# An agent-attention and maxout kernel: a rebuilt head, paired key-value additions, five relu slots, halved tiles and a newly searched instruction order

## The chip, the cores and the metric

The kernel runs on one core of a Trainium2 chip. Its time is device microseconds (us) of one execution. Before the change three runs gave a median of 438.29 us (437.61 to 439.87).

The core has five engines, each with its own in-order instruction queue: PE (matrix multiply; its weight loads are listed as PEld), ACT (activations), DVE (element-wise work), POOL (here: casts and additions in SBUF) and SP, which here only issues transfers (DMAs). PE writes into PSUM, which has 8 banks of 128 partitions x 512 fp32; ACT and DVE read from there.

## The reference, cut to what matters

```python
# q, k, v: (4, 12544, 128) fp32;  agents: (4, 49, 128);  w1, w2, w3: (128, 768);  w_out: (768, 128)
def _attn_ref(q, k, v, agents):
    scale = 1.0 / np.sqrt(q.shape[-1])
    def sm(a, b):                       # softmax over the last axis
        ...
    a2k = sm(agents, k)                 # 49 agents attend to 12544 keys
    agent_v = a2k @ v                   # (4, 49, 128)
    q2a = sm(q, agents)                 # each query attends to 49 agents
    return q2a @ agent_v
def _moe_ref(x, w1, w2, w3, w_out):
    h = np.maximum(np.maximum(x @ w1, x @ w2), x @ w3)
    return h @ w_out                    # x is the attention output, 50176 rows
```

## The kernel before, in words

**The algebra.** Each output row is a softmax mixture of 49 agent values, so the kernel multiplies agent values and weights once per batch: G = agent_v @ [w3-w1, w2-w1, w1 @ w_out], and then works from the 49 exponentials of a query instead of its 128 channels. With u = x(w3-w1) and v = x(w2-w1), max(xw1, xw2, xw3) = xw1 + max(relu(u), v). The part xw1 goes straight to the output through w1 @ w_out (the *linear* part).

**The head.** G of batch 0 must exist before any query can pass. The 98 key tiles and 98 value tiles (each 128 rows x 128) of batch 0 come in 12 chunks: ten of 9 tiles, two of 4 (`FIRST`). For chunk g the steps are `kl0.g` and `vl0.g` (loads, issued by SP), `kc0.g` (cast of the keys, POOL), `kt0.g` (transposes on PE into a PSUM pair, as 9 x 128 bf16 columns exceed one bank), `ke0.g` (out of PSUM, DVE), `ks0.g` (scores, PE), `kx0.g` (exp, ACT), `to0.g` (totals, PE), `vc0.g` (cast of the values, ACT), `kv0.g` (exponentials times values, PE, accumulated in one bank). Then `rs0`, `rc0`, `nr0` normalise the agent values into `avT` (DVE), the weights' differences `d31a` and so on are formed (DVE), `gpa` to `gpd` multiply (PE) and `gva` to `gvd` bring the pieces of G out of PSUM (two on ACT, two on DVE). `wm` and `wn` are matmuls of the identity with itself that compute nothing and keep PE busy.

**The stages.** 49 stages s of 8 query tiles (1024 queries) follow: `ql` (load), `qc` (cast, POOL), the transpose (either `qd`, a transposing DMA on SP, for the stages in `TURNED`, or `qt` on PE and `qe` on DVE), `sc` (scores), `ex` (exp on ACT into a tile EQ), `su` and `re` (sums and reciprocals). For each of the six 128-wide slices f of the hidden layer, `u.s.f` (PE) fills a pair of banks, `a.s.f` is its relu (ACT, into an SBUF slot of class AS, of which there are 3), `v.s.f` (PE) fills a second pair and `x.s.f` takes the maximum with AS into a tile of class R (DVE). For f = 4 (`FI`) both steps are on ACT and v is accumulated onto u's own pair. `p.s.o.f` multiplies R with w_out into two output banks, `li.s` adds the linear part, `ov.s.o` scales it into OS (DVE), `st.s` stores it. Where `SPLIT` has a `u`, u's tile is made in two single banks and its relu is two half instructions.

**Batches 1 to 3.** Their keys and values are handled in chunks of 9 tiles while the stages of the batch before run; there POOL casts both, SP turns the keys by DMA (`kt`), and `kv` adds its product into the same bank that holds the chunk's scores; `va` (DVE) adds this into an SBUF sum, once for each of 11 chunks.

**What sets the order.** `graph` lists all steps with their dependencies. The string `ORDER` lists them again in the order in which each engine's queue gets them, with the slot numbers (PSUM bank, SBUF buffer) after a slash. `Plan.waits` derives the semaphore waits from it. An engine that waits holds all that stands behind it in its queue. Every instruction is recorded in one helper, so every row of the profile has the line L388; rows are told apart by their tiles.

## Time and profile before

| | |
|---|---|
| time, median of 3 runs | 438.29 us (437.61 to 439.87) |
| profiled execution, first to last instruction | 436.6 us |
| that span below the median time | 1.7 us |
| PE, DVE, ACT, POOL busy | 94%, 89%, 90%, 39% |
| mean granted TensorE clock | 0.996 |
| DMA moved | 122.37 MB, mean 280 GB/s |

The page gives no device time for the profiled execution itself; its span lies 1.0 us below the fastest run. Names in a row read output<-input (`R<-ps,AS`: tile R is written from PSUM and AS), then the shape, the count, busy time and the mean of one. In a timeline row the numbers are the start and the duration in us, and a bracket tells how long the engine was idle before and what ended this. Under the heading of waits, a row tells who waited, for whose work, the total in us, how many times, and the longest.

### The profile page before, as it was taken

How to read it: one execution, taken by the hardware profiler on the slowest of the kernel's cores; microseconds unless marked ns; L12 is line 12 of the kernel's file. 1: busy time of each engine (PE TensorE's matmuls, PEld its weight loads, DVE VectorE, ACT ScalarE, POOL GpSimd, SP SyncE). 2: the span in 40 equal slices, each digit the busy share in tenths (PEclk: the TensorE clock that was granted, in tenths of full speed). 3: DMA queues.
4: the chain of work that ended last, by engine and by line, in shares of the span. 5: the costliest groups of instructions: out<-in, count | busy, mean ns of one | idle time of the engine just before them, and what ended most of it. 6: DMA issues, size and time to landing. Idle time of an engine off the chain costs nothing.

```text
span 436.6 us, 14853 instructions
## 1 busy us (share of the span) xinstructions
PE 411.9 (94%) x6488; PEld 256.9 (59%) x6488; DVE 386.6 (89%) x470; ACT 393.9 (90%) x486; POOL 170.0 (39%) x177
## 2 busy tenths in 40 slices
PE   1788999999999999999999999999999999999994
PEld 1464565666666566656656655656656555655574
DVE  1435999999999999999998999899999999999994
ACT  1278999999999999999999899999999999999993
POOL 3541565556655535165525445342531111000000
PEclk9989999999999999999999999999999999999999
DMA  8999999999999999999999999996999994266313
GB/s 310 411 410 383 311 334 372 289 281 343 269 318 342 279 371 298 266 339 285 294 345 261 407 247 278 276 326 143 276 363 290 284 306 98 74 208 208 119 71 125
DMA packets 98107, 122.37 MB, mean 280 GB/s; under 512 B 71479, under 2 KB 74235, under 8 KB 98043
## 3 DMA queue, kind: packets, MB, share of 16 engines
q1 hardware_dynamic: 97552, 121.07, 95.2%
q8 instruction: 51, 0.84, 0.8%
q10 hardware_dynamic: 491, 0.36, 0.3%
q14 instruction: 13, 0.11, 0.1%
HBM read 78.74 MB, written 25.69 MB: 239 GB/s over the span
## 4 chain that ended last, share of the span: by engine, by line
PE 69%; ACT 16%; DVE 7%; DMA 4%; issue 2%; POOL 1%; SPq 0%; POOLq 0%
PE ps L388 69%; ACT AS L388 9%; DVE R L388 6%; DMA LD<-in_k_dram 4%; ACT R L388 2%; ACT ps L388 2%; POOL KB L388 1%; DVE OS L388 1%; ACT EQ L388 1%; ACT VB L388 1%; ACT G L388 1%; ACT EK L388 1%; ACT OS L388 0%; SPq L388 0%; DVE QT L388 0%
## 5 line engine op out<-in xcount | busy, mean ns | idle before, releaser
L388 DVE TENSOR_TENSOR R<-ps,AS 128x1024 bf16<-128x1024 f32 x245 | 293.5, 1219 | 15.1 <-PE ps L388 10.7
L388 ACT ACTIVATE AS<-ps 128x1024 bf16<-128x1024 f32 (+1 forms) x259 | 245.8, 987 | 10.0 <-PE ps L388 7.2
L388 PE MATMUL ps<-EQ,G 49*128 49x512 bf16 (+1 forms) x1248 | 203.3, 370 | 3.5 <-ACT AS L388 0.7
L388 PE MATMUL ps<-wo_bf,R 64*128 64x128 bf16 (+1 forms) x3368 | 194.0, 218 | 1.1 <-issue 0.8
L388 PEld LDWEIGHTS ps<-wo_bf,R 64*128 64x128 bf16 (+1 forms) x3368 | 139.5, 95 | 59.4 <-issue 31.3
L388 PEld LDWEIGHTS ps<-EQ,G 49*128 49x128 bf16 x1248 | 56.4, 93 | 63.8 <-DVE R L388 18.3
L388 POOL CAST QB<-LD 128x1024 bf16<-128x1024 f32 x49 | 50.5, 1040 | 94.6 <-DMA QT<-QB 49.8
L388 POOL CAST KB<-LD 128x1152 bf16<-128x1152 f32 (+2 forms) x45 | 49.8, 1115 | 52.1 <-DMA LD<-in_k_dram 41.8
L388 DVE TENSOR_TENSOR OS<-ps,RC 128x512 f32<-128x512 f32 x96 | 65.4, 682 | 2.6 <-PE ps L388 2.2
L388 POOL CAST VB<-LD 128x1152 bf16<-128x1152 f32 (+1 forms) x33 | 37.4, 1136 | 40.7 <-DMA LD<-in_v_dram 36.5
L388 ACT ACTIVATE ps<-ps 128x1024 f32<-128x1024 f32 x49 | 49.9, 1018 | 2.8 <-PE ps L388 2.2
L388 ACT ACTIVATE R<-ps 128x1024 bf16<-128x1024 f32 x49 | 50.3, 1027 | 1.9 <-PE ps L388 1.6
L388 ACT ACTIVATE EK<-ps 128x441 bf16<-128x441 f32 (+2 forms) x45 | 23.4, 535 | 18.8 <-PE ps L388 18.4
L388 POOL TENSOR_TENSOR EA<-EA,EK 128x441 f32<-128x441 f32 x27 | 27.6, 1022 | 25.4 <-ACT EK L388 25.1
L388 ACT ACTIVATE EQ<-ps 128x512 bf16<-128x512 f32 x49 | 29.9, 610 | 1.0 <-PE ps L388 0.5
L388 DVE COPY KT<-ps 128x1152 bf16<-128x1152 bf16 (+1 forms) x12 | 8.2, 701 | 14.0 <-PE ps L388 14.0
L388 PE MATMUL ps<-QT,agT 128*64 128x512 bf16 (+1 forms) x104 | 19.9, 388 | 0.2
L388 PE MATMUL ps<-G,EQ 49*128 49x128 bf16 x392 | 19.1, 217 | 0.0
L388 PE MATMUL ps<-EK,VB 128*128 128x49 bf16 x392 | 17.4, 186 | 1.6 <-ACT VB L388 1.6
L388 PEld LDWEIGHTS ps<-EK,VB 128*128 128x128 bf16 x392 | 13.9, 97 | 8.1 <-ACT EK L388 4.2
L388 PE MATMUL ps<-agT,KT 128*128 128x49 bf16 x392 | 17.4, 186 | 0.4 <-DVE KT L388 0.4
L388 PEld LDWEIGHTS ps<-agT,KT 128*128 128x128 bf16 x392 | 14.4, 98 | 4.7 <-issue 2.1
(59 smaller groups left out, 177.6 us busy)
## 6 DMA issues: line engine op xcount, KB each, us to landing
LD<-in_q_dram SPq DMA_DIRECT2D x48, 512.0 KB, 7.7
out_dram<-OS SPq DMA_DIRECT2D x48, 512.0 KB, 6.2
LD<-in_k_dram SPq DMA_DIRECT2D x40, 576.0 KB, 7.6
...
KT<-KB SPq DMA_TRANSPOSE x33, 7.3
```

What stands on the lines that cost most here:

```text
L388: i = call(*args, **named)
```

## The change

- **Head.** Batch 0 comes in 13 chunks: twelve of 8 tiles and one of 2; 8 x 128 bf16 columns fit one PSUM bank. The value loads of chunks 0 to 9 land in OS buffers, the rest in LD, so that 23 buffers take loads where 13 did. The value casts are dealt out: 6 on POOL, 6 on ACT, 1 on DVE (`VCAST`). Exponentials of nine chunks live in R slots, the totals have a bank of their own, and the cast of w1 is on POOL. Each of w1, w2, w3 is loaded in three pieces (columns 0-127, 128-383, 384-767), and G of batch 0 is made in seven pieces a to f and l. 3 empty matmuls follow each value chunk (`AGAIN`) where 2 did.
- **Batches 1 to 3.** Scores and values have banks of their own; two chunks' products are accumulated before one `va`, 18 additions instead of 33.
- **Stages.** AS has 5 slots. `SPLIT` has four signs: `u` halves u and its relu, `v` halves v and its maximum, `b` both (and then each half of the maximum waits only for its own half of the relu). Of the 245 tiles outside f = 4, 77 have a halved u (14 before) and 74 a halved v (none before).
- **Transfers.** Stages 20, 21 and 23 are turned by DMA too: 31 instead of 28.
- **The order** is another one throughout, as are the slots. `ROWS` is another table: it says whether a product with w_out is issued on all 128 rows or as pairs on 64 rows. The linear part of G is stored in two zero-padded halves of 128 columns; the matmuls that read it have the same shape as before.

```diff
-FIRST = [KT] * 10 + [4, 4]
+AGAIN = (3,) * 13
+CUTS = {"a": (0, P), "b": (P, 3 * P), "c": (3 * P, DFF)}
+FIRST = [GT] * 12 + [2]
...
+VCAST = "pppaapapaaapd"
+CASTW = "p"
+OUTS = ("daaaadd", "addda", "addda", "adada")
...
-SLOTS = {"PS": 8, "LD": 13, ..., "AS": 3,
+SLOTS = {"PS": 8, "LD": 13, ..., "AS": 5,
...
-        add(f"vl0.{g}", SP, em.kv_load("v", 0, t0, n), new=[("LD", f"v0.{g}")], **dma(n * 65.536))
+        add(f"vl0.{g}", SP, em.kv_load("v", 0, t0, n), new=[("OS" if g < 10 else "LD", f"v0.{g}")], **dma(n * 65.536))
...
-        add(f"vc0.{g}", ACT, em.cast("v", "vb", 0, t0, n, ACT, 0, m), act(m * 128), after=[f"vl0.{g}"], new=[("VB", f"vb0.{g}")],
+        eng = ENGINES[VCAST[g]]
+        add(f"vc0.{g}", eng, em.cast("v", "vb", 0, t0, n, eng, 0, n), act(n * 128), after=[f"vl0.{g}"], new=[("VB", f"vb0.{g}")],
             use=[f"v0.{g}"])
...
-            add(f"va{r}", DVE, em.add_values(b, g, m), (0.13, 0.25), after=[f"kv{r}"] + ([f"va{b}.{g - 1}"] if g else []),
-                use=[m, plan.tile("VA", f"va{b}")])
+            if g % 2 or g == len(ch) - 1:
+                two = [(x, ch[x][1]) for x in range(g // 2 * 2, g + 1)]
+                y, h = f"{b}.{g // 2}", f"y{b}.{g // 2}"
+                add(f"kv{y}", PE, em.values(b, two, h), ...
+                add(f"va{y}", DVE, em.add_values(b, g // 2, h), ...
...
-                if two:
+                if SPLIT[s][f] in "ub":
                     us = [f"{u}.{h}" for h in range(2)]
...
+                if SPLIT[s][f] in "vb":
+                    vs = [f"{v}.{h}" for h in range(2)]
+                    add(v, PE, em.hidden(vs, s, f, C21, True), pe, mode=ROW, after=[f"ex.{s}"] + needs(1), new=[("PS", x) for x in vs],
+                        use=[e] + gs)
+                    for h in range(2):
+                        add(f"x.{s}.{f}.{h}", DVE, em.max_second(vs[h], s, f, h), (0.6, 0.72), after=[v, f"{a}.{h if SPLIT[s][f] == 'b' else 0}"],
+                            use=[vs[h], a, r])
...
 ORDER = """
-kl0.1/10 id0 kl0.3/6 kl0.11/9 id kl0.4/0 agl ones kc0.11/0 kl0.10/12 kc0.1/1 agc kc0.3/2 agt/1 prep kt0.1/0,1 kt0.3/2,3 wm.1/4
...
+id0 kl0.9/0 kc0.9/0 ones agl/0 agc/1 id wm.6/3 wm.0/0 agt/1 prep kt0.9/1 ke0.9/0 kl0.3/1 kl0.6/2 kc0.6/1 kt0.6/0 ke0.6/1 kc0.3/2 kt0.3/3
...
```

What the new order does is seen at three places. The first is SP's queue at the end of the head. Before, the last loads of batch 0's values (into LD buffers) and the weights behind them stood so:

```order
L388 DMA LD3_81<-in_v_dram 128x1152
L388 DMA LD12_90<-in_v_dram 128x1152
L388 DMA LD2_80<-in_v_dram 128x1152
L388 DMA LD4_82<-in_v_dram 128x1152
L388 DMA LD9_87<-in_moe_w3_dram 128x384
L388 DMA LD7_85<-in_moe_w1_dram 128x384 x2
L388 DMA LD0_78<-in_moe_w2_dram 128x384 x2
L388 DMA LD9_87<-in_moe_w3_dram 128x384
L388 DMA LD8_86<-in_q_dram 128x1024
```

Now, at the same place of SP's queue (OS names the output buffers that the values land in):

```order
L416 DMA LD3_77<-in_v_dram 128x1024
L416 DMA OS8_143<-in_v_dram 128x1024
L416 DMA OS9_144<-in_v_dram 128x1024
L416 DMA LD4_78<-in_moe_w1_dram 128x256
L416 DMA LD5_79<-in_moe_w3_dram 128x256
L416 DMA LD5_79<-in_moe_w3_dram 128x128
L416 DMA LD4_78<-in_moe_w1_dram 128x128
L416 DMA LD6_80<-in_moe_w2_dram 128x256
L416 DMA LD6_80<-in_moe_w2_dram 128x128
L416 DMA LD4_78<-in_moe_w1_dram 128x384
L416 DMA LD6_80<-in_moe_w2_dram 128x384
L416 DMA LD5_79<-in_moe_w3_dram 128x384
```

The first pieces of G need columns 0 to 383 of the weights, which now come ahead of the columns 384 to 767.

The second place is ACT's queue where the head ends. Before, with VB the cast values, EK and EQ exponentials, w_bf the cast of w1, G the pieces of G and AS the first relu:

```order
L388 ACTIVATE VB_99<-LD_90 128x1152
L388 ACTIVATE VB_100<-LD_80 128x1152
L388 ACTIVATE EQ_112<-ps 128x512
L388 ACTIVATE VB_97<-LD_82 128x1152
L388 ACTIVATE w_bf<-LD_85 128x768
L388 ACTIVATE G_147<-ps 128x384 x2
L388 ACTIVATE AS_117<-ps 128x1024
```

Now, ACT's queue over the same steps (R_128 holds exponentials of the keys here):

```order
L416 ACTIVATE R_128<-ps 128x392
L416 ACTIVATE EQ_105<-ps 128x512
L416 ACTIVATE EK_112<-ps 128x392
L416 ACTIVATE VB_93<-OS_140 128x1024
L416 ACTIVATE VB_94<-LD_77 128x1024
L416 ACTIVATE G_145<-ps 128x256
L416 ACTIVATE G_145<-ps 128x128
L416 ACTIVATE G_145<-ps 128x256
L416 ACTIVATE AS_113<-ps 128x1024
```

The last two value casts of the head (into OS8 and OS9) and the cast of w1 have left ACT for POOL, and ACT makes four pieces of G instead of two.

The third place is DVE's queue in the first stages, where R is a maximum, OS a scaled output, QT a copy of turned queries, VA an addition of the key-value sums. Before:

```order
L388 TENSOR_TENSOR R_131<-ps,AS_118 128x1024
L388 TENSOR_TENSOR OS_137<-ps,RC_135 128x4x128
L388 TENSOR_TENSOR R_126<-ps,AS_117 128x1024
L388 TENSOR_TENSOR OS_137<-ps,RC_135 128x4x128
L388 TENSOR_TENSOR R_128<-ps,AS_118 128x1024
L388 COPY QT_107<-ps 128x1024
L388 TENSOR_TENSOR R_122<-ps,AS_117 128x1024
L388 TENSOR_TENSOR VA_151<-ps,VA_151 128x49
```

Now, further on in the same stretch of DVE's queue:

```order
L416 COPY QT_103<-ps 128x1024
L416 TENSOR_TENSOR R_129<-ps,AS_117 128x512
L416 RECIPROCAL RC_133<-ps 128x16
L416 TENSOR_TENSOR R_129<-ps,AS_117 128x512
L416 TENSOR_TENSOR R_127<-ps,AS_113 128x512 x2
L416 TENSOR_TENSOR R_125<-ps,AS_114 128x1024
L416 TENSOR_TENSOR OS_139<-ps,RC_133 128x4x128
L416 TENSOR_TENSOR R_124<-ps,AS_115 128x512
L416 TENSOR_TENSOR VA_149<-ps,VA_149 128x49
L416 TENSOR_TENSOR R_124<-ps,AS_115 128x512
```

Single maxima have become two half instructions, with other work between them in two of the three cases.

More of the change, by code (lines that the diff above doesn't have):

```diff
@@ L63, in tile, with add @@
         return name
-    def add(self, name, eng, fn, cost, mode=FULL, after=(), new=(), use=(), serve=0.0, dma=False, sides=None):
+    def add(self, name, eng, fn, cost, mode=FULL, after=(), new=(), use=(), serve=0.0, dma=False, sides=None, lane=None):
         self.index[name] = len(self.ops)
@@ L233, in graph @@
+        add(f"to0.{g}", PE, em.totals(g, n), mm(1, n * 49), after=[f"kx0.{g}"], use=[f"e0.{g}", plan.tile("PS", "tot")])
+        eng = ENGINES[VCAST[g]]
+        add(f"vc0.{g}", eng, em.cast("v", "vb", 0, t0, n, eng, 0, n), act(n * 128), after=[f"vl0.{g}"], new=[("VB", f"vb0.{g}")],
             use=[f"v0.{g}"])
[L234 to L236 removed]
@@ new lines, in graph @@
+                add(f"a.{s}.{f}.0", ACT, em.relu(u, u, None), (0.917, 1.076), after=[u], use=[u])
+                add(v, PE, em.hidden([u], s, f, C21, False), pe, mode=ROW, after=[f"a.{s}.{f}.0"] + needs(1), use=[u, e] + gs)
+                if SPLIT[s][f] == "d":
+                    add(f"x.{s}.{f}.0", DVE, em.relu(r, u, None, DVE), (1.14, 1.28), after=[v], use=[u, r])
+                else:
+                    add(f"x.{s}.{f}.0", ACT, em.relu(r, u, None), (0.917, 1.076), after=[v], use=[u, r])
@@ L352, in graph @@
                 else:
-                    add(u, PE, em.hidden([u], s, f, C31, True), pe, mode=ROW, after=[f"ex.{s}"] + needs("a", "b"), new=[("PS", u, 3)], use=[e] + gs)
-                    add(a, ACT, em.relu(a, u, None), (0.917, 1.076), after=[u], use=[u, a])
-                add(v, PE, em.hidden([v], s, f, C21, True), pe, mode=ROW, after=[f"ex.{s}"] + needs("c", "d"), new=[("PS", v, 3)], use=[e] + gs)
-                add(f"x.{s}.{f}", DVE, em.max_second(v, s, f), (1.14, 1.28), after=[v] + ([f"{a}.{h}" for h in range(2)] if two else [a]),
-                    use=[v, a, r])
@@ L358, in graph @@
-        lin = ["gvl" if p[0] == 0 else f"gvl{p[0]}" for p in parts]
+                    add(u, PE, em.hidden([u], s, f, C31, True), pe, mode=ROW, after=[f"ex.{s}"] + needs(0), new=[("PS", u, 3)], use=[e] + gs)
+                    add(f"{a}.0", ACT, em.relu(a, u, None), (0.917, 1.076), after=[u], use=[u, a])
+                if SPLIT[s][f] in "vb":
[5 more added lines that the diff above has]
+                            use=[vs[h], a, r])
+                else:
+                    add(v, PE, em.hidden([v], s, f, C21, True), pe, mode=ROW, after=[f"ex.{s}"] + needs(1), new=[("PS", v, 3)], use=[e] + gs)
+                    add(f"x.{s}.{f}.0", DVE, em.max_second(v, s, f, None), (1.14, 1.28), after=[v] + [f"{a}.{h}" for h in range(1 + (SPLIT[s][f] == "u"))],
+                        use=[v, a, r])
@@ L359, in graph @@
+        lin = [f"gvl{p[0]}" for p in parts]
+        done = [[f"x.{s}.{f}.{h}" for h in range(1 + (f != FI and SPLIT[s][f] in "vb"))] for f in range(NF)]
         both = [plan.tile("PS", f"o.{s}.{o}") for o in range(2)]
         straight, turned = {both[0]: 0, both[1]: 1}, {both[0]: 1, both[1]: 0}
-        add(f"li.{s}", PE, em.out_linear(s), mm(4, 128), mode=ROW, after=[f"ex.{s}"] + lin, use=both + [f"e.{s}"] + gs, sides=straight)
+        if LINEAR[s] == "b":
+            add(f"li.{s}.0", PE, em.out_linear(s), mm(4, 128), mode=ROW, after=[f"ex.{s}"] + lin, use=both + [f"e.{s}"] + gs, sides=straight)
+        else:
+            for o in range(2):
+                add(f"li.{s}.{o}", PE, em.out_linear_half(s, o), mm(4, 128), after=[f"ex.{s}"] + lin, use=[both[o], f"e.{s}"] + gs)
@@ L463, in clear_ident, with clear_linear @@
         self.nc.gpsimd.memset(self.sides, 0.0)
+    def clear_linear(self):
+        for i in range(SLOTS["G"]):
+            self.nc.gpsimd.memset(self.slots["G", i][:, C1O:], 0.0)
     def make_ident(self):
```

648 lines of the change are left out of this document (342 added, 306 removed).

## The prediction

> **What bounds the kernel now.** I read first the page's span and busy times, then a table by stretches of the run. Its columns are start:end, length, then busy time (and instructions) of PE, PEld, DVE, ACT and POOL, the granted clock, the DMA share and GB/s.
>
> ```profile
> span 436.6 us, 14853 instructions
> ...
> PE 411.9 (94%) x6488; PEld 256.9 (59%) x6488; DVE 386.6 (89%) x470; ACT 393.9 (90%) x486; POOL 170.0 (39%) x177
> ```
>
> ```profile
> 0.00:35.00 35.00, 21.42 (x295) 15.67 (x296) 11.04 (x27) 14.12 (x21) 14.24 (x20) 0.95 0.96 379
> 35.00:45.00 10.00, 8.42 (x95) 4.14 (x94) 6.91 (x15) 9.32 (x13) 1.87 (x2) 1.00 1.06 382
> 45.00:425.00 380.00, 376.35 (x5952) 231.94 (x5952) 363.10 (x424) 365.54 (x447) 153.87 (x155) 1.00 0.98 273
> 425.00:436.60 11.60, 5.76 (x156) 5.17 (x152) 5.53 (x7) 4.90 (x8) 0.00 (x0) 1.00 0.39 142
> ```
>
> There are two regimes. Up to 35 us all compute engines are mostly idle and the DMA is full: a load-bound head. From 45 to 425 us DVE is busy 363.1 of 380 us (16.9 idle) and ACT 365.5 (14.5 idle). PE's busy time contains the latency of pipelined matmuls and says less. So I asked, for 45 to 425 us alone, who waits for whom:
>
> ```profile
> PEld ps L388 <- issue: 40.1, 161, 0.4
> ...
> PEld ps L388 <- DVE R L388: 18.6, 74, 0.6
> PEld ps L388 <- ACT AS L388: 15.4, 60, 0.4
> ...
> DVE R L388 <- PE ps L388: 10.7, 31, 0.7
> ...
> ACT AS L388 <- PE ps L388: 7.2, 22, 0.7
> ```
>
> PE's weight loads wait mostly for DVE's maxima and ACT's relus to empty a PSUM pair, and DVE and ACT wait mostly for PE to fill one. That is a ring through too few banks, with each engine near full; no row of that answer has PE, ACT or DVE waiting for a DMA. Both edges of the change lie here: the head (first 41 us) and the ring.
>
> **The head: -2.6 us.** What ends it stands in timelines of ACT, DVE and PE:
>
> ```profile
> 34.17 1.16 ACT L388 ACTIVATE VB<-LD 128x1152 bf16<-128x1152 f32 x1
> ...
> 35.89 2.21 ACT L388 ACTIVATE VB<-LD 128x1152 bf16<-128x1152 f32 x2
> 37.99 0.59 ACT L388 ACTIVATE EQ<-ps 128x512 bf16<-128x512 f32 x1
> 38.47 1.16 ACT L388 ACTIVATE VB<-LD 128x1152 bf16<-128x1152 f32 x1
> 39.66 0.84 ACT L388 ACTIVATE w_bf<-LD 128x768 bf16<-128x768 f32 x1
> ```
>
> ```profile
> 39.12 0.56 DVE L388 TENSOR_TENSOR wall<-LD,LD 128x384 bf16<-128x384 f32 x1 [0.70 <-DMA LD<-in_moe_w_dram]
> 40.13 0.21 DVE L388 TENSOR_TENSOR avT<-ps,KR 128x49 bf16<-128x49 f32 x1 [0.45 <-PE ps L388]
> ```
>
> ```profile
> 41.41 0.60 PE L388 MATMUL ps<-EQ,G 49*128 49x512 bf16 x4
> ```
>
> ```profile
> L388 POOL CAST QB<-LD 128x1024 bf16<-128x1024 f32 x49 | 50.5, 1040 | 94.6 <-DMA QT<-QB 49.8 <-DMA LD<-in_q_dram 42.4 <-PE ps L388 2.1
> ```
>
> The last value cast ends at 38.47 + 1.16 = 39.63, and ACT shows no idle bracket there: its queue is late, not the load. Keys and values of batch 0 are 2 x 12544 x 128 x 4 = 12.85 MB, with agents 0.10 and the first queries 0.52: 13.47 MB. By 35 us 35 x 379 GB/s = 13.27 MB are in, the rest at 35.5. How late does a landing count? Before, the weights bring it to 14.65 MB, by bytes at 35 + 1.38/0.382 = 38.6; DVE was released at 39.12. So I add 0.5: the last values count at 36.0.
>
> Now that cast is on POOL: 1.04 us (the row of QB has its shape), done at 37.1. From the end of the cast to the first matmul of stage 0 took 41.41 - 39.63 = 1.78 us; I keep that: 38.8, a gain of 2.6. The weights must agree: the first u needs two pieces, 0.26 MB, at 36.7 with the 0.5, before avT is ready. All six early pieces (0.59 MB) count at 37.6; with a difference (0.56) and the 1.28 from avT to the first u they allow v by 39.4, while the first relu is still running. The last three pieces land near 39.1, as before, for f = 3 to 5.
>
> Bounds: 1.5 us if the first u must await all six pieces as it did before, since only 0.59 MB went behind it (0.59/0.382); 3.1 without the 0.5. POOL takes 6 value casts (6.2 us), the cast of w1 (0.84) and small clears; it was busy 14.2 of 35 us, which hides them. Without that cover the last cast starts up to one cast, 1.04 us, later. One transpose into one bank instead of two, 13 chunks, and 15 more empty matmuls are work on engines with 14 to 24 idle us: nothing on the path.
>
> **The stages: loads.** Back-to-back starts give the true cost of an instruction, its record being longer than the distance to the next:
>
> ```profile
> 64.13 1.22 DVE L388 TENSOR_TENSOR R<-ps,AS 128x1024 bf16<-128x1024 f32 x1
> 65.26 0.68 DVE L388 TENSOR_TENSOR OS<-ps,RC 128x512 f32<-128x512 f32 x1
> 65.86 0.68 DVE L388 COPY QT<-ps 128x1024 bf16<-128x1024 bf16 x1
> 66.48 0.26 DVE L388 RECIPROCAL RC<-ps 128x16 f32<-128x16 f32 x1
> ...
> 67.83 0.21 DVE L388 TENSOR_TENSOR VA<-ps,VA 128x49 f32<-128x49 f32 x1
> 67.95 3.71 DVE L388 TENSOR_TENSOR R<-ps,AS 128x1024 bf16<-128x1024 f32 x3
> ```
>
> ```profile
> 50.72 1.08 ACT L388 ACTIVATE AS<-ps 128x512 bf16<-128x512 f32 x2 [0.28 <-PE ps L388]
> ...
> 63.78 1.02 ACT L388 ACTIVATE AS<-ps 128x1024 bf16<-128x1024 f32 x1
> 64.69 1.03 ACT L388 ACTIVATE R<-ps 128x1024 bf16<-128x1024 f32 x1
> ```
>
> - DVE: a whole maximum takes 1.13 (65.26 - 64.13), a half about 0.60 (the OS row, the nearest shape). 74 halved: 74 x 0.07 = +5.2. 15 fewer additions VA at 0.12: -1.8. 3 fewer copies QT at 0.6: -1.8. Net +1.6.
> - ACT: a whole relu takes 0.91; two halves record 1.08 together and one 0.60, so a half takes 0.48. 63 more halved: 63 x 0.05 = +3.2.
> - PE: along its list from stage 0 on, the matmuls change between whole-array and split forms 482 times instead of 441, about a quarter microsecond each where it shows (40.1/161, the row on issue; 161 of 441 showed): +3.7; three PE transposes fewer give back 1.8, at 0.61 for the 8 matmuls of one in PE's timeline:
>
> ```profile
> 49.33 0.61 PE L388 MATMUL ps<-ident,QB 128*128 128x128 bf16 x8
> ```
>
> This hides while PE is not the last to be ready; where it is, PE's 1.9 come on top.
>
> **The stages: banks.** Groups by shape, with mean ns:
>
> ```profile
> L388 DVE TENSOR_TENSOR R<-ps,AS 128x1024 bf16<-128x1024 f32 x245 | 293.5, 1219 | 15.1 <-PE ps L388 10.7 <-ACT AS L388 1.2
> L388 ACT ACTIVATE AS<-ps 128x1024 bf16<-128x1024 f32 x231 | 230.9, 1033 | 7.8 <-PE ps L388 5.2
> ...
> L388 PE MATMUL ps<-EQ,G 49*128 49x512 bf16 x1152 | 198.8, 383 | 3.5 <-ACT AS L388 0.7 <-DVE R L388 0.5 <-ACT ps L388 0.3
> ...
> L388 DVE TENSOR_TENSOR OS<-ps,RC 128x512 f32<-128x512 f32 x96 | 65.4, 682 | 2.6 <-PE ps L388 2.2
> ...
> L388 ACT ACTIVATE AS<-ps 128x512 bf16<-128x512 f32 x28 | 15.4, 604 | 2.2 <-PE ps L388 2.0
> ```
>
> A u tile holds its pair 0.38 + 1.03 = 1.41 us. Halved, the first bank is free at 0.98, the second at 1.46: mean 1.22, 0.19 less. A v tile goes from 1.60 to a mean of 1.36 (1.06 and 1.66), 0.24 less. 63 x 0.19 + 74 x 0.24 = 29.7 pair-us; with two banks as outputs there are three pairs, so 9.9 us of the run at most. What can be won is bounded again by the idle time: 14.5 less 3.2 on ACT, 11.3.
>
> The other end: no idle goes and ACT's 3.2 lies on the path; +3.2. Which value? 74 of 245 maxima, 30%, are halved. If DVE's idle time shrinks by that share, 0.30 x 16.9 = 5.1, less its extra 1.6, the stages gain 3.5. I take -3.5: the waits on R and AS average 0.25 us, less than the half instruction by which a halved tile frees its first bank. ACT must then go from 14.5 idle to 380 - 3.5 - 368.7 = 7.8; possible, not generous.
>
> The Trainium skill speaks against the halving: Perfetto Trace Analysis, section Optimizing Scalar/DVE Operations, gives a fixed overhead per instruction of about 125 ns for DVE on PSUM and says that grouping helps where the engine is saturated, breaking up where it is not and makes others wait. By that figure DVE's toll would be an estimated 74 x 0.125 = 9.3 us, and the sum 4.1 us worse than mine. The trace's 0.07 per halved maximum says less; and DVE at 96% with PE waiting for it fits both halves of the advice.
>
> The issue row has a quarter microsecond of idle 161 times. The Trainium skill, TensorEngine Tiling (Array Packing), section Key Properties, says that changing the tiling mode drains the engine. By that, every one of the 41 more changes costs, an estimated 10 us of PE time instead of 3.7, and the sum would be that much worse only if PE were the last to be ready throughout. The trace agrees with the drain, not with its being on the path: 280 of 441 changes show nothing.
>
> **The rest.** No row shows ACT or POOL held by DVE's use of AS, so five slots alone free nothing; they let the list put relus further ahead. Three more turning transfers stand in SP's queue, each waiting for POOL's cast, with loads and stores behind them:
>
> ```profile
> SPq L388 <- POOL QB L388: 41.3, 13, 7.6
> ```
>
> With 13 such waits at 28 turns, three more add some 4.4 us of SP's time (41.3/28 x 3). Nobody on PE waits for loads in this stretch, so zero; if the stores and loads behind had no lead, those 4.4 us. The tail has the same work: zero, half a microsecond either way.
>
> **Sum.** -2.6 - 3.5 = -6.1: a span of 430.5. The span before lies 1.7 under the median of the runs, so the time is 438.3 - 6.1 = 432.2 us. A measurement of this kernel can tell 0.5%, 2.2 us, from no change.
>
> **Rivals.**
> - *The toll decides (slower).* Each half instruction pays what its record shows: ACT 2 x 0.604 - 1.033 = 0.175, times 63 = 11.0 us. ACT at 365.5 + 11.0 = 376.5 of 380 becomes the bound and, if its 14.5 idle us stay, the stages grow by 11.0: 438.3 - 2.6 + 11.0 = 446.7; with half of the idle time gone (7.3), 439.4; the middle, 443. It decides once the toll that is not covered passes 2.6 us. For it: ACT is the fullest engine. Against: starts lie 0.48 apart, not 0.60. Chance 0.13.
> - *The head alone.* The bank time freed is eaten by halves and mode changes: 438.3 - 2.6 = 435.7. For it: all three loads grow. Against: the waits on R and AS are the commonest. Chance 0.20, split evenly over the line at 0.5%.
> - *The ring opens.* The bank time counts in full: -9.9 and the head's 2.6: 425.8. For it: visible idle is put down to PE almost alone. Against: ACT's ceiling. Chance 0.13.
> - *The head does not shorten*, the weights or POOL's last cast ending it where ACT did: 438.3 - 3.5 = 434.8. Against: 0.59 MB less ahead of the first u. Chance 0.05.
>
> The forecast keeps 0.49. Faster: 0.49 less 0.02 for a forecast that falls short, 0.13 of the ring and 0.10 of the head alone, 0.03 of the last: 0.73. Slower: the toll's 0.13 and 0.01 of the head alone. Same: the rest, 0.09 + 0.02 + 0.02 = 0.13. The range reaches from 425 (the ring opens, with the head's 3.1) to 440.5 (the toll half covered); about 2 in 10 lie outside.
>
> **What would show it.** Right: the first matmul EQ,G near 38.8; the last value cast on POOL ending near 37; DVE idle in the 380 us after the head near 12; waits of PEld on R and AS below 34 us. Wrong: ACT's idle unchanged with busy time above 370, rows of PE waiting for DMA QT or LD, or the first u after 40.

## The result, and the profile after

The kernel after the change took 443.21 us in the median of three runs (441.3 to 443.91), beside 438.02 for the kernel before on the same chip (four runs): a ratio of 1.0104 (95% interval 1.0069 to 1.0138). Taken again on another chip (a_again below) it took 441.53 (440.22 to 443.48), a ratio of 1.0061 (1.0039 to 1.0084). So it is slower by 0.6 to 1.0%; forecast was 6.1 us faster. A fourth run of the first set, 447.99 us, lies over 1.5% above the fastest and is left out here, as are three others of that kind below.

The profiled run is the fastest of the three, 441.3 us, with a span of 438.9; before's span was 436.6. The page of after, with the queue that brings instructions (q8) and the shares of the chain that ended last:

```profile
span 438.9 us, 14876 instructions
...
PE 412.0 (94%) x6404; PEld 257.2 (59%) x6404; DVE 388.4 (88%) x532; ACT 389.1 (89%) x545; POOL 177.7 (40%) x189
...
q8 instruction: 50, 0.82, 0.8%
...
PE 61%; ACT 15%; DMA 14%; DVE 4%; issue 3%; POOL 2%; SPq 0%; POOLq 0%; DVEq 0%
PE ps L416 61%; ACT AS L416 8%; DMA LD<-in_q_dram 6%; DMA KT<-KB 4%; DVE R L416 3%; DMA LD<-in_moe_w_dram 2%; ACT R L416 2%; ACT ps L416 2%; DMA LD<-in_k_dram 1%; POOL KB L416 1%; ACT EQ L416 1%; DVE OS L416 1%; POOL QB L416 1%; ACT EK L416 0%; ACT G L416 0%
```

The busy times of PE, DVE and ACT are those of before within 5 us; POOL's is 7.7 us more. DMA had 4% of before's chain and has 14% of this one: by the last line 4% are transfers into KT, and the rest are loads, which this chain meets up to 49.5 us, in the head and just behind it. The table by stretches, columns as in the prediction:

```profile
0.00:35.00 35.00, 23.09 (x314) 16.13 (x314) 11.33 (x27) 12.17 (x20) 19.43 (x29) 1.00 0.96 378
35.00:45.00 10.00, 9.06 (x92) 4.26 (x90) 6.98 (x17) 5.66 (x10) 4.54 (x6) 1.00 1.07 374
45.00:425.00 380.00, 372.95 (x5804) 230.59 (x5804) 363.56 (x484) 365.49 (x509) 153.75 (x156) 1.00 0.96 271
425.00:438.90 13.90, 6.89 (x206) 6.26 (x200) 6.48 (x8) 5.74 (x9) 0.00 (x0) 0.85 0.58 221
```

DVE is idle for 16.4 of the 380 us (before 16.9, forecast 12) and ACT for 14.5, as before. Who waits for whom there:

```profile
PEld ps L416 <- issue: 43.7, 173, 0.6
...
PEld ps L416 <- ACT AS L416: 16.9, 65, 0.5
PEld ps L416 <- DVE R L416: 14.1, 54, 0.5
...
DVE R L416 <- PE ps L416: 8.3, 24, 0.6
...
ACT AS L416 <- PE ps L416: 4.4, 15, 0.6
PEld ps L416 <- DMA KT<-KB: 4.0, 3, 1.8
ACT EK L416 <- PE ps L416: 3.6, 4, 1.1
...
DVE OS L416 <- PE ps L416: 2.5, 3, 1.4
```

The waits that the change was to shorten did shorten: DVE for PE at a maximum from 10.7 to 8.3, ACT for PE at a relu from 7.2 to 4.4. In their place stand new ones: PE's weight loads wait 4.0 us for KT, the turned keys of the next batch, and ACT (at EK, 3.6 us, before 0.4) and DVE (at OS, 2.5 us, before 0.5) wait for PE while it stands. On PE it is three stands:

```profile
53.46 0.40 PE L416 MATMUL ps<-agT,KT 128*128 128x49 bf16 x9 [0.68 <-DMA KT<-KB]
58.33 0.40 PE L416 MATMUL ps<-agT,KT 128*128 128x49 bf16 x9 [1.39 <-DMA KT<-KB]
...
106.23 0.40 PE L416 MATMUL ps<-agT,KT 128*128 128x49 bf16 x9 [1.18 <-DMA KT<-KB]
```

Four marks cut the run into pieces: the first u, the first scaled output of stage 1, the end of the last maximum, the end of the span. In the timelines of after (PE, DVE) and of before (DVE, ACT):

```profile
40.86 0.60 PE L416 MATMUL ps<-EQ,G 49*128 49x512 bf16 x4
...
65.33 0.69 DVE L416 TENSOR_TENSOR OS<-ps,RC 128x512 f32<-128x512 f32 x1 [0.18 <-PE ps L416]
...
429.58 1.21 DVE L416 TENSOR_TENSOR R<-ps,AS 128x1024 bf16<-128x1024 f32 x1
```

```profile
63.53 0.68 DVE L388 TENSOR_TENSOR OS<-ps,RC 128x512 f32<-128x512 f32 x1
...
429.47 1.02 ACT L388 ACTIVATE R<-ps 128x1024 bf16<-128x1024 f32 x1 [1.61 <-PE ps L388]
```

| from - to | before | after | difference | forecast |
|---|---|---|---|---|
| start - first u | 41.41 | 40.86 | -0.55 | -2.6 |
| - scaled output of stage 1 | 22.12 | 24.47 | +2.35 | with the next row: -3.5 |
| - last maximum done | 366.96 | 365.46 | -1.5 | |
| - end of the span | 6.11 | 8.11 | +2.0 | 0 |

(Last maximum done: 429.58 + 1.21 = 430.79 after, 429.47 + 1.02 = 430.49 before.) The four sum to +2.3, the difference of the spans. The long middle gained, and the pieces around it lose two and a half times as much. Before, too, PE stands once where nothing in the profile holds it ("issue"), just ahead of its third mark, so a part of the third row may be this stand:

```profile
428.83 0.38 PE L388 MATMUL ps<-wo_bf,R 64*128 64x128 bf16 x7 [0.79 <-issue]
```

By the scaled outputs next to it on DVE, which was busy without a stand there, the middle is 2.0 us shorter (65.33 to 428.98 after, 63.53 to 429.15 before). The marks account for the 2.3 us of this run, not for the further 2 us of the median.

### The profile page after: what moved, and what is told of

Same layout as the page of the kernel before. It is cut to its first block, busy times and chain, and to the rows that moved or that the text cites. A ratio compares the mean times of both kernels' runs of the same rounds, so it can differ in the third digit from the quotient of the medians.

```text
span 438.9 us, 14876 instructions
## 1 busy us (share of the span) xinstructions
PE 412.0 (94%) x6404; PEld 257.2 (59%) x6404; DVE 388.4 (88%) x532; ACT 389.1 (89%) x545; POOL 177.7 (40%) x189
## 4 chain that ended last, share of the span: by engine, by line
PE 61%; ACT 15%; DMA 14%; DVE 4%; issue 3%; POOL 2%; SPq 0%; POOLq 0%; DVEq 0%
PE ps L416 61%; ACT AS L416 8%; DMA LD<-in_q_dram 6%; DMA KT<-KB 4%; DVE R L416 3%; DMA LD<-in_moe_w_dram 2%; ACT R L416 2%; ACT ps L416 2%; DMA LD<-in_k_dram 1%; POOL KB L416 1%; ACT EQ L416 1%; DVE OS L416 1%; POOL QB L416 1%; ACT EK L416 0%; ACT G L416 0%
## 5 line engine op out<-in xcount | busy, mean ns | idle before, releaser
L416 DVE TENSOR_TENSOR R<-ps,AS 128x1024 bf16<-128x1024 f32 (+1 forms) x319 | 297.5, 970 | 12.4 <-PE ps L416 8.3
L416 ACT ACTIVATE AS<-ps 128x1024 bf16<-128x1024 f32 (+1 forms) x322 | 249.8, 834 | 7.5 <-PE ps L416 4.4
L416 PEld LDWEIGHTS ps<-wo_bf,R 64*128 64x128 bf16 (+1 forms) x3294 | 141.1, 95 | 61.7 <-issue 34.7
L416 PEld LDWEIGHTS ps<-EQ,G 49*128 49x128 bf16 x1248 | 57.4, 93 | 61.3 <-ACT AS L416 12.5
L416 ACT ACTIVATE R<-ps 128x1024 bf16<-128x1024 f32 (+1 forms) x58 | 54.6, 946 | 4.9 <-PE ps L416 4.8
L416 ACT ACTIVATE EK<-ps 128x441 bf16<-128x441 f32 (+2 forms) x37 | 19.7, 539 | 17.8 <-PE ps L416 17.5
L416 PE MATMUL ps<-ident 128*128 128x512 bf16 x47 | 13.3, 389 | 7.4 <-POOL ident L416 6.5
L416 DVE COPY KT<-ps 128x1024 bf16<-128x1024 bf16 (+1 forms) x13 | 8.3, 658 | 12.0 <-PE ps L416 12.0
L416 PEld LDWEIGHTS ps<-G,EQ 49*128 49x128 bf16 x392 | 13.6, 94 | 4.8 <-ACT EQ L416 1.2
## 6 DMA issues: line engine op xcount, KB each, us to landing
OS<-in_v_dram SPq DMA_DIRECT2D x10, 512.0 KB, 16.4
```

What stands on the lines that cost most here:

```text
L416: i = call(*args, **named)
```

## The experiments

My theory after seeing the traces has three parts. **Landing**: a load is there when the slowest of 16 DMA engines has it, and that set the end of the head. **Turnings**: a turning transfer waits for every load queued ahead of it, and the new order has PE arrive first. **Code**: PE's own instructions come by DMA, and at the end they were queued behind stores. The main rival is the prediction's: halves and changes of form cost their toll throughout.

**1. b_pool: the step of the head.** In before, one engine is exchanged:

```diff
-        add(f"vc0.{g}", ACT, em.cast("v", "vb", 0, t0, n, ACT, 0, m), ...
+        eng = POOL if g == 7 else ACT
+        add(f"vc0.{g}", eng, em.cast("v", "vb", 0, t0, n, eng, 0, m), ...
```

> The kernel before with one change: the last value cast of batch 0 is on POOL instead of ACT. The prediction's reading (the load counts at 36.0, ACT's queue was late): the cast on POOL ends near 37.1, avT and the first matmul EQ,G come up to 2.6 us earlier, at 38.8. Landing theory (the slowest of the 16 DMA engines has the last value chunk at 38.05): the cast runs 38.1 to 39.2 behind a wait for the load, the first matmul EQ,G comes at about 40.9, 0.5 us earlier.

The timelines of POOL and PE in b_pool:

```profile
37.97 1.15 POOL L389 CAST VB<-LD 128x1152 bf16<-128x1152 f32 x1 [4.86 <-DMA LD<-in_v_dram]
...
41.07 0.60 PE L389 MATMUL ps<-EQ,G 49*128 49x512 bf16 x4
```

POOL stood free for 4.86 us and was released by the load, at 37.97. The first u came 0.34 us earlier than 41.41, not 2.6; 438.13 us (one run). The load was late; ACT's queue was behind it by 0.4 us only.

**2. a_code: why the load is late.** The trace notes each of the 16 engines' landings. Taken together (first and last engine of the last value chunk; PE fetches with its start, all in us):

```
            first engine  last engine   fetches of PE code before 34 us
before         35.52         38.05       two, the second at 33.0
after          35.72         38.11       18.5 and 30.5
a_code         35.69         38.49       17.4, 25.5 and 32.4
```

The first engine has it when the bytes say (the prediction's 35.5). In after the distance to the last is 0.8 us up to the first fetch, 1.75 behind it, and 2.3 to 2.4 behind the second; in before 1.0, 1.9 to 2.0, and 2.5 to 2.6. a_code adds a fetch:

```diff
+            if name in ("warm.5", "warm.4", "warn.5", "warn.11"):
+                for _ in range(32):
+                    self.nc.tensor.matmul(self.t[name][:, 0:32], self.ident, self.ident[:, 0:32], ...
```

> The kernel after, with 128 narrow empty matmuls more (32 columns, 256 records with their weight loads) in four places of the head, from about 9 to 22 us, in PE's idle time. Code theory (each fetch of PE code, 16 KB and 1.0 us, delays one of the 16 DMA engines, and a load is there when the slowest engine has it): three fetches fall before 33 us instead of two, the last value chunk of batch 0 is complete near 39.0 instead of 38.11, the first matmul EQ,G near 41.8 instead of 40.86. Rival (the late landing has nothing to do with PE's code): the last value chunk at 38.1, the first matmul EQ,G at 40.9.

POOL's cast of the last value chunk and the first u in a_code:

```profile
38.54 1.04 POOL L416 CAST VB<-OS 128x1024 bf16<-128x1024 f32 x1 [0.35 <-DMA OS<-in_v_dram]
...
41.81 0.61 PE L416 MATMUL ps<-EQ,G 49*128 49x512 bf16 x4
```

The third fetch fell at 32.4, and the last chunk landed 0.4 later than in after, not 0.9. Nor did the added fetch bring this: in a_code the distance is 1.1 before any fetch, 2.7 behind the first, still 2.7 behind the second, and 2.7 to 2.8 behind the third. The first u moved by the 0.95 expected, of which the added work on PE may be a part. So the distance is shown to be what makes the load late; that fetches make the distance is seen in the steps right behind most of them, but a_code does not show that one more adds to it.

**3. a_stores and a_fewer: the end.** PE in after, at the end, and the DMA queues from 426.5 to 429 and from 430.3 to 431.3 (packets, MB, share of the 16 engines):

```profile
429.88 1.39 PE L416 MATMUL ps<-wo_bf,R 64*128 64x128 bf16 x24
432.80 0.62 PE L416 MATMUL ps<-wo_bf,R 128*128 128x128 bf16 x8 [1.53 <-issue]
```

```profile
q1 hardware_dynamic: 275, 1.00, 102.6%
```

```profile
q1 hardware_dynamic: 77, 0.31, 79.0%
q8 instruction: 1, 0.02, 5.5%
```

Nothing that the profile shows held PE for 1.53 us. But q8 brought a packet of 16 KB from 430.37 to 431.24: 256 of PE's 13014 records, the last 21 of which are the matmuls and weight loads that came late. In all traces a fetch starts between 0.7 us before and 6.2 us after PE enters the piece before it, so I take that entry as the request, to within some tenths. Here it entered at 426.93 and needed the next at 431.05; the request stood 3.44 us behind four stores that had been issued from 423.95 on. Two edits remove this in different ways, one at the stores, one 400 us earlier:

```diff
 a_stores (ORDER)
-... qd.46/1 qd.47/3 ... st.46 st.39 st.41 ... st.37 ...
+... qd.46/1 qd.47/3 st.37 st.39 st.41 ... st.46 ...
 a_fewer
-AGAIN = (3,) * 13
+AGAIN = (1,) * 13
```

> The kernel after, with the stores of stages 37, 39 and 41 put in SP's queue behind the turning transfer of stage 47 instead of behind the store of stage 46; nothing else. Code theory (PE stands 1.53 us at 431 because the last piece of its own instructions, which comes by DMA, was queued behind four stores issued from 423.95 to 425.64): the fetch follows its request by under 2 us, the gap of PE before its last 8 matmuls falls from 1.53 to under 0.3, the span from 438.9 to about 437.4. Rival (the gap belongs to the change of matmul form or to the last maxima): the gap stays 1.5 and the span 438.9.

> The kernel after, with one empty matmul after each value chunk of the head instead of three: 26 matmuls and 26 weight loads fewer, all before 41 us, nothing else. Code theory (PE's instructions come in pieces of 256; the gap at 431 lies at a border of two pieces, 21 records before PE's end): with 52 records fewer the border falls behind PE's last instruction, the gap at the end goes, span about 437.4, although nothing near the end is changed; the head keeps two fetches and its first matmul EQ,G within 0.3 us of 40.86. Rival (stores or form at the end make the gap): it stays at 1.5, span 438.9.

PE at the end, a_stores and then a_fewer:

```profile
429.28 1.83 PE L416 MATMUL ps<-wo_bf,R 64*128 64x128 bf16 x32
```

```profile
430.93 1.83 PE L416 MATMUL ps<-wo_bf,R 64*128 64x128 bf16 x32
```

In both the last matmuls run through without a stand. In a_stores the fetch started at 427.09, 0.77 us behind its request; span 436.6, time 438.57 (437.18 to 442.14; ratio to before 1.0022, 0.9995 to 1.0049). Of the 2.3 us of span, 1.7 arise at the end. In a_fewer the gap vanished though nothing near the end is changed: the border of two pieces had moved behind PE's last instruction. A third sign: counted from PE's first record, the stands marked "issue" of after (record 12993), before (12993) and a_fin (7361, below) begin at the same place in a piece, 193 past a multiple of 256. So the code theory holds at the end.

a_fewer's time, 441.76 (437.48 to 443.68; ratio 1.0057, 1.0024 to 1.0091), is no gain for all that. Its table by stretches shows something else (the third number from the right is the granted clock):

```profile
36.00:40.00 4.00, 2.37 (x39) 1.42 (x41) 1.85 (x7) 0.33 (x2) 2.08 (x2) 1.00 1.09 365
40.00:44.00 4.00, 3.87 (x23) 1.05 (x23) 3.30 (x8) 3.89 (x7) 1.58 (x2) 0.73 1.08 374
44.00:48.00 4.00, 4.00 (x27) 1.84 (x24) 3.85 (x6) 2.85 (x6) 3.33 (x5) 0.50 1.03 410
48.00:52.00 4.00, 4.00 (x28) 2.26 (x29) 2.22 (x4) 2.50 (x5) 2.00 (x2) 0.50 1.15 270
```

With fewer empty matmuls PE was busy 2.37 of 4 us at 36, and then ran at half speed from 41.8 to 52.1, in the first stages. Its first scaled output came 2.05 us later than after's, but from 108 to 187 us it was level with after's or up to 0.4 ahead, and a new stand for code, 0.70 us at 284.64, took a part of the gain at the end; the span is 438.2. Why most of its ten runs, all with mean clocks of 0.979 to 0.991, took 441 us and more is not shown.

The Trainium skill, Runtime: NRT & Kernel Launch, section Instruction fetch mechanics, says that an engine's instructions are refilled in blocks of 16 KiB (256 instructions) over the sequencer's own DMA queue, and that crossing a block costs "one DMA tail-bump, mostly hidden". Block and queue agree with the trace. Hidden are most crossings here too; the one with 3.44 us of queue ahead cost 1.53 us.

**4. a_turns, a_mix, a_swap, b_loads: the turnings.** In after the second turning of batch 1 was issued at 49.83 and landed at 58.28; in before, issued behind the first with no load between, 49.02 and 52.57. The load between (k2) landed at 54.90; why the turning took 3.4 us more, where it took 1.0 behind another turning, is not explained. Orders of SP's queue (k, v, q: loads of keys, values, queries; T: turnings):

```
before   v0 q3 T0 T1 v1 ...
after    q3 v1 v0 T0 k2 T1 ...
a_turns  T0 T1 q3 v1 v0 k2 ...   (and two loads of batch 2 behind the turning of chunk 8)
a_mix    v1 v0 T0 T1 q3 k2 ...   (POOL's cast of q3 moved along)
a_swap   q3 v1 v0 T0 T1 k2 ...   (POOL's cast of k2 behind the casts of v1, v0)
b_loads  v0 q3 v1 T0 k2 T1 ...   (before, with the loads where after has them)
```

a_mix and a_swap start from a_stores.

> The kernel after, with the turning transfers of the first two key chunks of batch 1 moved ahead of four loads in SP's queue, and two loads of batch 2 moved behind the turning of chunk 8. Theory of the transfers (a turning transfer waits for all loads queued ahead of it, and PE waits for it): PE's waits for KT at 52.6, 56.6 and 104.8 (4.0 us together) shrink to under 1 us, the first scaled output at 65.3 comes 1.5 to 2 us earlier, the span goes to about 437. Rival (the early stages lose by the toll of half instructions): the output at 65.3 moves by less than 0.5 us and the span stays at 438.9.

> The kernel with the three stores moved (a_stores, profiled span 436.6), and besides: in SP's queue the two turnings of the first key chunks of batch 1 now stand back to back directly behind the loads of the two value chunks, the load of stage 3's queries and that of key chunk 2 behind them. Theory of the transfers (PE's waits for KT at 52 and 56 us, 2.7 us, come from loads that stand between and ahead of the turnings; the values themselves must stay ahead, as a_turns showed): the second turning lands near 54.5 instead of 57.8, PE's waits for KT before 60 us fall under 1 us, the first scaled output of stage 1 (64.8 in a_stores) comes 1.5 to 2.5 us earlier, span 434 to 435. Rival (those waits cover others that are late as well: PE's next products wait for the values' casts on POOL): the output moves by under 0.5 us, span 436.6.

> a_stores (profiled span 436.6; ten runs, 437.2 to 438.8 where the mean clock was 0.998 or more, 441.0 to 442.1 where it was 0.993 or less) with one swap on SP and one on POOL: the second turning of batch 1 directly behind the first, ahead of the load of key chunk 2; that chunk's cast behind the two value casts. Theory of the transfers: the second turning lands near 54.0 instead of 57.8, PE's wait of 1.40 us at 57.8 goes, the first scaled output of stage 1 comes 1.4 to 2 us earlier than 64.8; span 434.6 to 435.3; and since PE no longer stands there, no run has the lower clock, so the median is near 436.5. Rival (something else is late next, by as much): 436.6 and a median of 438.5.

> The kernel before with two loads moved in SP's queue to where the kernel after has them: the second value chunk of batch 1 ahead of the first turning, key chunk 2 between the first and the second. Theory of the transfers: the first turning lands 1.3 us later than 51.56, the second near 56 to 57 instead of 52.57, PE gets waits for KT of 1 to 3 us before 60 us, span 437.5 to 440. Rival (PE has other work ahead and the transfers are hidden): no wait for KT above 0.3 us, span 436.6.

PE in a_turns, with its table by stretches, and PE in a_mix:

```profile
63.45 0.64 PE L416 MATMUL ps<-EK,VB 128*128 128x49 bf16 x18 [4.14 <-POOL VB L416]
```

```profile
60.00:64.00 4.00, 0.55 (x18) 0.53 (x18) 0.00 (x0) 0.44 (x1) 3.93 (x4) 1.00 1.02 291
64.00:68.00 4.00, 4.00 (x56) 2.61 (x52) 2.78 (x5) 1.86 (x3) 2.52 (x4) 0.57 1.09 226
```

```profile
56.68 0.61 PE L416 MATMUL ps<-ident,QB 128*128 128x128 bf16 x8 [0.93 <-ACT R L416]
60.37 0.64 PE L416 MATMUL ps<-EK,VB 128*128 128x49 bf16 x18 [1.67 <-POOL VB L416]
```

The waits for KT up to 60 us went in a_turns and a_mix, and worse ones came: the first product of keys with values now needs two value chunks (the paired additions), and these had been pushed back. a_turns took 444.73 us, ratio 1.014, with a span of 442.6 where 437 was expected. a_mix took 441.59, 1.0078, span 439.2 where 434 to 435 was expected; but there the early loss was not what counted. Its scaled output of stage 1 came 1.8 later than in a_stores, that of 150 us 0.1 later; the 2.7 us of span arose at one stand for code:

```profile
256.86 0.18 PE L416 MATMUL ps<-agT,KT 128*128 128x49 bf16 x1 [2.43 <-issue]
```

The fetch before it (record 7361 again) had started 5.8 us behind its request. a_swap took the stand at 58 away without a new one there; that at 53 stayed, 0.70 us. Its scaled output of stage 1 came at 63.9 instead of 64.8, less than the 1.4 of the stand; from there to 240 us its outputs came between 0.1 later and 1.6 earlier than those of a_stores, at 240 us 1.1 earlier. Then the lead was lost: DVE stood 1.03 us for a store to free an output buffer, PE 1.03 us for a value cast of batch 3, late on POOL.

```profile
245.72 0.69 DVE L416 TENSOR_TENSOR OS<-ps,RC 128x512 f32<-128x512 f32 x1 [1.03 <-DMA out_dram<-OS]
```

```profile
246.95 0.62 PE L416 MATMUL ps<-EK,VB 128*128 128x49 bf16 x18 [1.03 <-POOL VB L416]
```

Span and time came out at 436.9 (expected: 434.6 to 435.3) and, in the median, 438.75 (ratio 1.0011, 0.9987 to 1.0035). b_loads gives the counter test: the turnings landed at 53.28 and 57.19, the scaled output of stage 1 came 0.9 later, the span grew by 1.2, and the time was 439.94, slower than before by 0.25% (0.12 to 0.38). PE waited only 0.64 us for KT there, where 1 to 3 us were expected.

In a_turns the clock went to half speed for 3.4 us behind a stretch in which PE was busy 0.55 of 4 us; in a_mix, from 61.3 on, it did so too. The Trainium skill, TensorE: Matmul & The Clock Gate, section What's actually happening, says that PE's clock falls to half after an idle window of about 3.4 us that runs freely, not from the kernel's start. The length agrees with the 3.41 us of the half-speed stretches here; but in a_mix no stand was that long: in the 3.41 us before its stretch PE stood once for 1.67 us and was busy 1.75.

**5. a_again, a_keep, a_clock: is it the clock that makes a part of the runs longer?** Of ten runs of a_stores, six took 437.2 to 438.8 at a mean clock of 0.998 or more, four 441.0 to 442.1 at 0.993 or less. Two edits of a_stores put six empty matmuls where PE stands, one at 57 us, one at 22 us in the head:

```diff
 a_keep
-... kc1.2/1 v.1.2/2,3 x.1.2.0/10 kt1.1/0 ks1.1/7 ...
+... x.1.2.0/10 kt1.1/0 wm.8/4 wm.9/5 wm.10/6 wm.11/0 wm.12/1 wm.13/4 ks1.1/7 ...
 a_clock
-... kc0.10/0 kt0.10/0 ...
+... kc0.10/0 wm.8/6 wm.9/6 wm.10/6 wm.11/6 wm.12/6 wm.13/6 kt0.10/0 ...
```

> a_stores with six empty matmuls (identity, 1.3 us) in PE's queue right ahead of the scores of key chunk 1, where PE otherwise stands 1.40 us until the turning has landed. Clock theory (where PE stands too long between 52 and 60 us, its clock is halved for 3.4 us, in some runs; a_turns and a_mix show such a stretch at 64.0 and 61.3): the profiled span stays 436.6 within 0.5, but of ten runs none or one has a mean clock of 0.994 or less, where a_stores had four of ten; median 438.3, highest under 440. Rival (the 3 us of the slower runs have another cause): four of ten near 441 to 442.

> a_stores with six empty matmuls (1.3 us) ahead of the transposes of key chunk 10, where PE stands 1.1 us at 22 us for a cast on POOL (2.0 us in a_keep's trace, in which a half-speed stretch followed at 23.76). Clock theory (a stand of PE there is followed, in part of the runs, by half speed from 23 to 27 us, which makes the head 1.3 us longer): of twelve runs at most two have a mean clock of 0.992 or less, where a_stores had three of ten and a_keep three of twelve; profiled span 436.6, median 438.3. Rival (the slower runs come from stretches elsewhere): three or more of twelve stay at 441 or above.

> The kernel after, unchanged, in more runs, to see how its runs spread beside the two kernels below. If the clock makes the spread: runs with a mean clock of 0.994 or more near 441, those below 0.992 near 443 to 445. If it doesn't: no order by the clock.

a_keep: 440.17 (ratio 1.0033, 1.0015 to 1.0051), four of twelve runs still at 0.993 or less; in its trace, span 440.1, no half-speed stretch follows 57 us, but two stand in the head, at 23.76 and 44.24. So filling the stand at 57 us does not keep such stretches away; a_swap, without it, had runs at 0.994 and 0.988 too, which was not expected. a_clock: 438.73 (ratio 1.0009, 0.9987 to 1.0031), ten of twelve runs from 437.75 to 439.54, one at 0.988 with 443.21, but also one at 0.997 with 441.36. That is within what the clock theory asks for, on few runs, and its profiled run still had a stretch at half speed, from 58.4 to 61.9. The eight runs of a_again do not follow their clock: 440.22 at 0.996, 441.57 at 0.985, 443.0 at 0.997. The last is the profiled one, and its trace names another cause. Up to 140 us it is level with after's trace or ahead; then it loses 2.0 us at one stand, which is more than the whole 1.9 between the two spans:

```profile
151.96 0.64 PE L416 MATMUL ps<-EK,VB 128*128 128x49 bf16 x18 [2.04 <-POOL VB L416]
```

In after's trace the same product runs at 150.03 without a stand. The value load behind it had its first engine at 146.84 and its last at 149.61; in after's trace these were 146.02 and 146.78. So the clock may be a part of the spread, and the drift of the 16 engines is another; how much each makes in the other runs stays open.

**6. a_swhole and a_sqt: the change's own parts.** a_swhole undoes 83 of 151 halvings in `SPLIT`; a_sqt takes stages 20, 21 and 23 out of `TURNED`:

```diff
 a_sqt (ORDER)
-... qc.20/0 qd.20/0 ... qd.21/2 ... qd.23/1 ...
+... qc.20/0 ... qt.20/3 qe.20/0 ... qt.23/1 qe.23/1 ... qt.21/1 qe.21/2 ...
```

> a_stores with 43 of the 77 halved relus and 40 of the 74 halved maxima made whole again (all whose two banks are neighbours), at the place of their first half. Ring theory (halving frees banks earlier: forecast -3.5 us for all): without 55% of it the stages are longer by 1.5 to 4 us, span 438 to 440.5. Toll theory (each half costs 0.05 on ACT and 0.07 on DVE on the path): 43 x 0.05 + 40 x 0.07 = 4.9 us of engine time less, span 432 to 435.

> a_stores with stages 20, 21 and 23 turned on PE again (transposes into a free bank, copy on DVE) instead of by DMA. Forecast of the prediction: the three turning transfers cost nothing, while three transposes on PE (0.61 us each) and three copies on DVE (0.6 each) cost up to 1.8 us: span 436.6 to 438.4. Rival (the transfers stop the other loads, 4.4 us of SP's time): span 433 to 436.

a_swhole took 448.67 us (ratio 1.0243, 1.0216 to 1.0269; span 447.3, +10.7 on a_stores), a_sqt 444.53 (1.0148; span 442.8, +6.2). Both lie above every span that was expected. The waits of a_swhole from 45 to 425 us:

```profile
PEld ps L416 <- ACT AS L416: 19.8, 63, 0.7
PEld ps L416 <- DVE R L416: 17.3, 57, 0.8
DVE R L416 <- PE ps L416: 14.8, 40, 0.7
ACT AS L416 <- PE ps L416: 10.8, 29, 0.8
```

With fewer half instructions all four ring waits grow, from 42.7 us together in a_stores (16.7, 13.2, 8.5 and 4.3) to 62.7, and the loss grows over the whole run. This speaks against the toll as an account of after's loss: with 83 halvings less nothing came back. It is not a clean test: this order was searched with the halves in it, and a whole tile at the place of its first half may wait longer than one for which an order is made. The same holds for a_sqt, where 4.4 us arise between 190 and 199 us (from 189 to 210 POOL waited 4.8 us for PE's transposes to free the cast queries) and 1.6 of the rest earlier, in places that the edit does not touch. What the three turnings are worth in themselves is not settled.

**7. a_best, a_slack, a_fin: is the sum of PE's stands the missing gain?** Three kernels on top of a_swap with a_clock's empty matmuls. All cast value chunk 0 of batch 3 ahead of chunk 1; besides, a_best loads chunk 1 earlier, a_slack puts PE's steps later, and a_fin moves loads of batch 2:

```diff
 a_best
-... vl3.5/12 kl3.5/5 vl3.1/7 ... vc3.1/3 qc.27/1 qc.26/0 kc3.5/1 vc3.0/1 ...
+... vl3.1/7 vl3.5/12 kl3.5/5 ... vc3.0/1 vc3.1/3 qc.27/1 qc.26/0 kc3.5/1 ...
 a_slack: ks1.0 kx1.0 and kv2.0 va2.0 and kv3.0 va3.0 eight PE steps later, ks1.7 kx1.7 five
 a_fin
-... vl2.2/12 kl2.0/8 kt1.7/2 vl1.8/2 qd.10/2 kt1.8/3 ... kt2.4/0 ... kt2.3/1 ... kt2.2/3 qd.13/2 ... vl2.0/0 ...
+... kt1.7/2 vl1.8/2 qd.10/2 kt1.8/3 vl2.2/12 kl2.0/8 ... vl2.0/0 kt2.4/0 ... kt2.3/1 ... kt2.2/3 qd.13/2 ...
```

> All that has helped together: a_stores, the swap of the second turning (a_swap: 0.9 us earlier from 64 to 237 us, given back at 245 us where POOL cast the long landed value chunk 0 of batch 3 behind four others and PE waited 1.03 us for it), and now that cast first, its neighbour's load three places ahead, and the six empty matmuls of a_clock. Theory of the transfers: no wait for VB on PE near 246, the 0.9 us are kept to the end, span 435.5, median of the runs with a mean clock of 0.995 or more near 437.3. Rival (the stretch from 230 to 255 us is full of transfers, 2.4 us behind on the slowest engine, and takes back what comes early): scaled output near 246.9 as in a_stores and span 436.6.

> a_swap with the six empty matmuls of a_clock and the cast of value chunk 0 of batch 3 ahead of chunk 1's, and now, in PE's own order, the scores of key chunks 0 and 7 of batch 1 (8 and 5 PE steps) and the first value products of batches 2 and 3 (8 steps each, with their additions on DVE) put later: the places where PE stood 0.7 to 1.4 us for KT or for VB in the traces of after, a_stores, a_swap and a_best. Theory (the order has PE arrive at those products before their transfers and casts are there; the stages themselves are 2 us shorter than before's): no stand of PE of 0.9 us or more between 45 and 425 us, span 434 to 435.5, median 436 to 437, below before's 438.6. Rival (the time given back is set elsewhere: engines' loads, transfers): stands gone, span still 436 to 437.5, median 438 to 439.

> The other way to take those stands away: PE's order as in a_swap, the transfers earlier instead. a_swap with the six empty matmuls of a_clock, the cast of value chunk 0 of batch 3 ahead of chunk 1's, two loads of batch 2 behind the turning of chunk 8 (as in a_turns), and the load of value chunk 0 of batch 2 ahead of four turnings instead of behind them. Theory: the stands at 105, 150 and 247 go without new ones, span 434.5 to 435.8, median 436.5 to 437.5, below before's 438.5. Rival (what comes early is taken back elsewhere): span 436.5 to 438, median 438 to 439.5.

PE's new stands, in a_best, a_slack and a_fin:

```profile
104.70 0.40 PE L416 MATMUL ps<-agT,KT 128*128 128x49 bf16 x9 [1.14 <-DMA KT<-KB]
150.21 0.64 PE L416 MATMUL ps<-EK,VB 128*128 128x49 bf16 x18 [1.24 <-POOL VB L416]
```

```profile
107.34 0.64 PE L416 MATMUL ps<-EK,VB 128*128 128x49 bf16 x18 [1.70 <-ACT EK L416]
```

```profile
255.27 0.31 PE L416 MATMUL ps<-agT,KT 128*128 128x49 bf16 x6 [0.75 <-issue]
```

a_best took 439.79 us (ratio 1.0022, 1.0003 to 1.004; span 437.3), a_slack 442.03 (1.0075; 441.0), a_fin 439.55 (1.0028, 1.0005 to 1.0051; 437.8); spans of 434 to 435.8 had been expected. Each took away stands it aimed at and met others. In a_slack a stretch at half speed followed the stand at 107.34, from 108.46 on, and together they cost 3.6 us against a_swap. a_fin was 0.8 us ahead of a_stores at 110 us and 0.4 at 246, and 1.2 us behind at 264; of the 1.6 us between, 1.0 came where PE stood for its own code again, at 255.27, behind a fetch that had waited 4.22 us in its queue. No version here beats before; the best, a_stores, a_swap and a_clock, are level with it. That the sum of the stands would be the gain is not shown.

## Why the prediction was wrong

- **The head, -2.6: the step that failed first.** "Its queue is late, not the load" was read off a missing idle bracket on ACT. The bracket was missing because an exponential filled the time until 38.47; the load had landed at 38.05. And "the last values count at 36.0" took the bytes of all 16 engines and half a microsecond, where the slowest engine was 2.5 us behind the first. The half microsecond came from a row that was set against the wrong bytes: DVE's release at 39.12 was compared with all six weight pieces (14.65 MB, 38.6), but that difference needs only the first two, which landed at 38.58 and 39.10; with them 13.86 MB are in, by the same rate at 36.5. So the row says 2.6 us late, not 0.5. b_pool shows the step: 0.34 gained by that cast's move. The rest of the chain came out: in after the load counted at 38.11, and with the prediction's own 1.04 for the cast and 1.78 to the first u this gives 40.9; it came at 40.86. Measured for the whole head: 0.55 gained.
- **No wait of PE for a load or a turning, zero: failed.** "No row has PE, ACT or DVE waiting for a DMA" was true of before's order and was carried over to an order whose last lines I had seen only on SP, ACT and DVE, not where PE's scores of the next batch stand against the turnings of their keys. The three more turnings, stages 20, 21 and 23, were not what failed: the stands lie at 53, 58 and 106 us. Two signs of being wrong that the prediction named came true: PE waiting for a transfer, with KT instead of QT or LD, and the first u after 40. Up to stage 1 the run lost 2.35, with 2.07 of PE's stands for KT in it; taking the longer of the two away (1.39) gave back 0.96.
- **The tail, zero within half a microsecond: failed**, by +2.0. The stand for code there is 1.53, and 1.7 went with it in a_stores; what the rest is stays open. The amount of work was the same, as said; where three stores stood in SP's queue was not.
- **The stages, -3.5: right in kind, mis-sized.** The waits on R and AS fell to 31.0 (forecast: under 34), those of DVE and ACT for PE by 5.2, and from stage 1 to the end of the stages the run gained 1.5 to 2.0 (2.1 in a_stores, by the scaled outputs). DVE's idle time fell by 0.5 only, where 5.1 was forecast. Why no more came of it is open, and which part of the change brought the gain is not separated. The price of 41 more changes of form, +3.7 of PE's time on "issue", came out: 43.7 instead of 40.1.
- **The toll** (the rival on the slower side, 0.13): the sign came out as it said; that this was its mechanism is not borne out. Much of the loss lies at stands, and a_swhole is slower with 83 halvings less. The advice of the Trainium skill, Perfetto Trace Analysis, section Optimizing Scalar/DVE Operations, to group where an engine is saturated found no support here: the kernel with fewer halves took 448.67 us, in an order searched for more.
- **Code and clock** were in none of my rivals.
